# Routing's running sums on TensorE, and three reordered steps, in an attention and expert kernel

## The chip, the cores and the metric

The kernel runs on one core of a Trainium2 chip. A core has TensorE (PE in the profile, with its weight loads as PEld), VectorE (DVE), ScalarE (ACT), GpSimd (POOL) and SyncE (SP), which here issues most of the DMA transfers. The metric is the device time of one execution in microseconds.

## The reference

Eight images are each run through an attention of 8 heads (576 tokens, 64 channels a head) with an additive bias per head, and the result goes through a layer of 8 experts, of which each token takes one.

```python
scores = scale * np.matmul(q, k.transpose(0, 1, 3, 2))
h = np.maximum(x @ w1 + b1, 0.0)          # x from the distance of two positions
scores = scores + (h @ w2).transpose(2, 0, 1)[None]
attn = np.exp(scores - scores.max(-1)); attn = attn / (attn.sum(-1) + 1e-9)
out = attn @ v                            # reshaped to 4608 tokens x 512
...
logits = x @ w_gate + modality_bias[modality_id]
e_idx = np.argmax(logits, axis=1)
gate_w = softmax(logits)[arange(N), e_idx]
out[e_idx == e] = gate_w * (relu(x @ w1[e]) @ w2[e])   # for each expert e, F = 1024
```

## The kernel before

The program has three stages. The **table stage** (to about 66 us) computes the attention's bias for every distance: 32 blocks of hidden values (rows of `relu`, made by VectorE at L185 and ScalarE at L183), a product with `w2` on TensorE (L193), a copy out of the accumulator (`bias_put`, L209 on ScalarE) into a ring of four buffers, and a transfer to the table (SP's queue, L212). Among the blocks, a list of steps prepares the first pair of heads: `turn` (L378, VectorE) transposes q and k, and `split` (L385, L386) divides each into an upper part, ScalarE's cast, and a lower part, a subtraction that reads that cast. `SPLIT0 = (6, 10)` names the blocks behind which the two splits of pair 0 are issued.

The **attention** runs 32 pairs of heads, four to an image, one after the other, and each in five units of 128 (the last 64) query rows. What is issued in a unit is written out by hand in `ORDER`, one string per unit, a letter per step: S scores (L402) with VectorE's reduction for the row minimum (L416), e and f the exponentials of the two heads (ScalarE, L431), t and T the transposes of the exponentials of heads 1 and 2 (L446) from the block scored two units before, a, A, b, c the products with v (L500), R the transposes of the remainders (L474), X and B one step each of the routing. t writes the accumulator bank `eps_716`, T `eps_717`; the copy ("take") from the bank to `eT` is ScalarE's (L331) where `ON_ACT` names it (among others e11, e20, e21, e30: block and head) and VectorE's (L333) elsewhere. A digit behind a letter holds the take back by so many steps, but it is issued before its bank is written again. In unit 4, t and T handle block 2 (e20, e21); in unit 0 of the next pair, e30 and e31; in unit 1, block 4 (L452, bank 716). Every engine runs its instructions in the order in which they are issued.

The **routing** of an image runs as a list of steps spread over the next image's four pairs. I number an image's pairs 4k to 4k+3; the routing of the image before takes place from unit 4 of pair 4k to the end of pair 4k+3. Of interest here: in pair 4k+2 `s_top` in unit 0 (bias, maximum, subtraction, L784 to L787), `s_onehot` in unit 1 (L793 to L803), `s_rank` in unit 2 (each token's place among those of its expert: a product of the one-hot rows with a triangle of ones, and a product of running sums over the five blocks of rows with a matrix of ones, L816 and L817), then `s_gate` (L807 to L812) and in unit 3 `s_pos` (L828, L830), whose places GpSimd's scatter reads. The step of the last image runs at the start of the third stage.

The **expert layers** (from about 614 us) gather the tokens of each expert and run the two products.

The change touches `split`, `ORDER[4]`, `s_top`, `s_onehot`, `s_gate`, `s_rank` and `s_pos`.

Of the kernel before, what the change touches and what calls it, by code (L numbers as in the profile page):

```python
# [11 lines left out]
F32 = mybir.dt.float32  # L12
BF16 = mybir.dt.bfloat16
F32R = mybir.dt.float32r
I32 = mybir.dt.int32
AF = mybir.ActivationFunctionType
ALU = mybir.AluOpType
# [4 lines left out]
P = 128  # L22
S = 576
# [6 lines left out]
E = 8  # L30
# [78 lines left out]
class Attn:  # L109
# [270 lines left out]
    def split(self, n, part):  # L380

        nc = self.nc
        x, cols = (self.kT, slice(0, NK)) if part else (self.qT, slice(NK, NK + NQ))
        hi, lo = self.QK[n % 2][:, 0, cols], self.QK[n % 2][:, 1, cols]
        nc.scalar.copy(hi, x)  # L385
        nc.gpsimd.tensor_tensor(lo, x, hi.bitcast(F32), op=ALU.subtract)  # L386

    def scores(self, n, c):

# [127 lines left out]
    def first_steps(self, route):  # L517
# [31 lines left out]
    )  # L549

    def attention(self):
# [64 lines left out]
    def route_setup(self, cp):  # L616

        tc, nc, io = self.tc, self.nc, self.io
        B = self.B
        NC = 5 * B  # L620
        self.n_tab = -(-self.n_tok // TS) * TS + TS
        self.xg = self.dp.tile([(E + 1) * self.n_tab, XW], F32, name="xg")

        self.ones = cp.tile([P, P], BF16, name="ones")
        nc.gpsimd.memset(self.ones, 1.0)
        self.wgb = cp.tile([P, NP, 2, 16], F32, name="wgb")
        nc.gpsimd.memset(self.wgb, 0.0)

        self.lt4 = cp.tile([P, P], F32, name="lt4")
        nc.gpsimd.memset(self.lt4[:, 64:P], 0.0)  # L630
        self.rec = cp.tile([P, 5, H], F32, name="rec")
        nc.gpsimd.memset(self.rec, 1.0)
        self.oh = cp.tile([P, 6, E], F32, name="oh")
        nc.gpsimd.memset(self.oh, 0.0)
        self.ohb = cp.tile([P, 2, 6, E], BF16, name="ohb")
        nc.gpsimd.memset(self.ohb, 0.0)
        yield
        self.base = cp.tile([P, E], F32, name="base")
        nc.sync.dma_start(self.base, io["c_ebase"].to_broadcast([P, E]))
        yield  # L640
        blank = cp.tile([P, 2, XW], F32, name="blank")
        nc.gpsimd.memset(blank[:, :, 0:DM], 0.0)
        nc.gpsimd.memset(blank[:, :, DM:XW], float(self.n_tok))
        self.blank = blank
        self.gi = cp.tile([P, 5, 4], F32, name="gi")
        nc.gpsimd.memset(self.gi, 0.0)
        self.ids = cp.tile([P, NC], F32, name="ids")
        nc.sync.dma_start(self.ids, io["c_ids"])
        yield
        self.valid = cp.tile([P, 5], F32, name="valid")  # L650
        nc.sync.dma_start(self.valid, io["c_valid"])
        yield
        self.rev = cp.tile([P, E], F32, name="rev")
        nc.sync.dma_start(self.rev, io["c_rev"].to_broadcast([P, E]))
        yield
        wg = io["moe_w_gate"]
        for h in range(2):
            sl = slice(64 * h, 64 * h + 64)
            nc.sync.dma_start(
                self.wgb[sl, :, h, 0:E], wg.rearrange("(p a d) e -> a d p e", a=2, d=D)[h]  # L660
            )
            yield

        x0, x1 = self.xrb

        m2 = x0[:, 0 : 2 * NC].bitcast(I32).rearrange("p (b c w) -> p b c w", b=B, c=5)
        nc.gpsimd.memset(m2, 0)
        yield
        mid = io["moe_modality_id"].bitcast(I32)
        for c in range(4):  # L670
            nc.sync.dma_start(
                m2[:, :, c, :],
                mid.rearrange("(b s) -> b s", s=2 * S)[:, 2 * P * c : 2 * P * c + 2 * P].rearrange("b (p w) -> p b w", p=P),
            )
        yield
        nc.sync.dma_start(
            m2[0:64, :, 4, :], mid.rearrange("(b s) -> b s", s=2 * S)[:, 1024 : 2 * S].rearrange("b (p w) -> p b w", w=2)
        )
        yield
        tri = x1[:, 0:P]  # L680
        nc.sync.dma_start(tri, io["c_tri"])
        yield
        mb = x1[:, P : P + 2 * E].rearrange("p (a e) -> p a e", a=2)
        nc.sync.dma_start(
            mb.rearrange("p a e -> p (a e)"),
            io["moe_modality_bias"].rearrange("a (o e) -> o (a e)", o=1).to_broadcast([P, 2 * E]),
        )
        yield
        yield
        self.tri = cp.tile([P, P], BF16, name="tri")  # L690
        nc.gpsimd.tensor_copy(self.tri, tri)
        mf, m1 = x0[:, 2 * NC : 3 * NC], x0[:, 3 * NC : 4 * NC]
        nc.gpsimd.tensor_copy(mf, m2.rearrange("p b c w -> p (b c) w")[:, :, 0])
        nc.gpsimd.tensor_scalar(m1, mf, -1.0, 1.0, op0=ALU.mult, op1=ALU.add)
        self.mbias = cp.tile([P, NC, E], F32, name="mbias")
        yield
        t0 = x0[:, 4 * NC : 12 * NC].rearrange("p (n e) -> p n e", e=E)
        for a, (dst, mk) in enumerate(((t0, m1), (self.mbias, mf))):
            nc.gpsimd.tensor_tensor(
                dst,  # L700
                mk.rearrange("p (n o) -> p n o", o=1).to_broadcast([P, NC, E]),
                mb[:, a : a + 1, :].to_broadcast([P, NC, E]),
                op=ALU.mult,
            )
        yield
        nc.gpsimd.tensor_tensor(self.mbias, self.mbias, t0, op=ALU.add)

    def route_steps(self, b):
        nc, rt = self.nc, self.rt
        xT = [self.xT.pop(NP * b + p) for p in range(NP)]  # L710
        sums = [self.sums.pop(NP * b + p) for p in range(NP)]
        rec, oh = self.rec, self.oh
        C5 = [P, 5, E]
        st = {}

        def bc(t):
            return t.rearrange("p (c o) -> p c o", o=1).to_broadcast(C5)
# [64 lines left out]
        def s_top():  # L782
            lg = st["lg"]
            nc.vector.tensor_tensor(lg, lg, self.mbias[:, 5 * b : 5 * b + 5, :], op=ALU.add)  # L784
            mx = rt.tile([P, 5], F32, tag="mx", name=f"mx{b}")
            nc.vector.tensor_reduce(mx, lg, axis=AX.X, op=ALU.max)
            nc.vector.tensor_tensor(lg, lg, bc(mx), op=ALU.subtract)  # L787
            st["mx"] = mx

        def s_onehot():  # L790
            lg, mx = st["lg"], st["mx"]

            nc.vector.scalar_tensor_tensor(  # L793
                oh[:, 0:5, :], lg, 0.0, self.rev.rearrange("p (o e) -> p o e", o=1).to_broadcast(C5), op0=ALU.is_ge, op1=ALU.mult
            )
            nc.vector.tensor_reduce(mx, oh[:, 0:5, :], axis=AX.X, op=ALU.max)
            nc.vector.tensor_tensor(oh[:, 0:5, :], oh[:, 0:5, :], bc(mx), op=ALU.is_equal)
            nc.vector.tensor_tensor(oh[:, 0:5, :], oh[:, 0:5, :], bc(self.valid), op=ALU.mult)

            ohb = self.ohb  # L800
            nc.gpsimd.tensor_copy(ohb[:, 0, 0:5, :], oh[:, 0:5, :])
            for k in range(1, 6):
                nc.vector.tensor_tensor(ohb[:, 1, k, :], ohb[:, 1, k - 1, :], oh[:, k - 1, :], op=ALU.add)  # L803

        def s_gate():
            lg = st["lg"]
            nc.scalar.activation(lg, lg, AF.Exp)  # L807
            gt = rt.tile([P, 5], F32, tag="gt", name=f"gt{b}")
            nc.vector.tensor_reduce(gt, lg, axis=AX.X, op=ALU.add)
            nc.vector.tensor_scalar(gt, gt, 1e-9, None, op0=ALU.add)  # L810
            nc.vector.reciprocal(self.gi[:, :, 0], gt)
            nc.vector.tensor_copy(self.gi[:, :, 1], self.ids[:, 5 * b : 5 * b + 5])  # L812

        def s_rank():
            ps = self.xbank()[:, 0 : 6 * E].rearrange("p (c e) -> p c e", e=E)
            nc.tensor.matmul(ps, self.tri, self.ohb[:, 0], start=True, stop=False)  # L816
            nc.tensor.matmul(ps, self.ones, self.ohb[:, 1], start=False, stop=True)  # L817
            rk = rt.tile(C5, F32, tag="rk", name=f"rks{b}")
            bb = self.base.rearrange("p (o e) -> p o e", o=1)
            nc.vector.tensor_tensor(rk, ps[:, 0:5, :], bb.to_broadcast(C5), op=ALU.add)  # L820
            nc.vector.tensor_tensor(self.base, self.base, ps[:, 5, :], op=ALU.add)
            nc.vector.tensor_tensor(rk, rk, oh[:, 0:5, :], op=ALU.mult)
            st["rk"] = rk

        def s_pos():
            rk = st["rk"]
            pf = rt.tile([P, 5], F32, tag="pf", name=f"pf{b}")
            nc.vector.tensor_reduce(pf, rk, axis=AX.X, op=ALU.add)  # L828
            pos = rt.tile([P, 5], I32, tag="pos", name=f"pos{b}", bufs=2)
            nc.vector.tensor_copy(pos, pf)  # L830
            st["pos"] = pos

        def s_rows(c):
# [611 lines left out]
```

## Time and profile before

| | |
|---|---|
| median of 3 runs | 1062.39 us |
| lowest and highest | 1062.15 and 1063.95 us |
| the profiled execution's own time | 1062.4 us |
| its span in the trace | 1060.5 us |
| granted TensorE clock, share of full speed | 0.998 |
| busy, share of the span: PE, DVE, ACT, POOL | 95%, 70%, 63%, 29% |

The profile shows one execution. The span goes from the first to the last instruction of the trace and is 1.9 us shorter than the execution's own time. A row of a timeline groups neighbouring instructions of one kind: start, time from the first's start to the last's end, what they are, their count, and in brackets the idle time before them with what ended it. Rows overlap a little, since an instruction starts before the one before it has drained.

### The profile page before, as it was taken

The page shows a single profiled execution, that of the slowest core. Times are in us where ns is not written, and L with a number is a line of the kernel's source. Part 1 is how long each engine was busy: PE and PEld are TensorE (multiplying, and loading weights), DVE is VectorE, ACT ScalarE, POOL GpSimd, SP SyncE. Part 2 cuts the span into 40 slices and gives each one's busy share as a digit, 9 for nine tenths or more (in the row PEclk, how much of TensorE's full clock was granted, in tenths as well). Part 3 has the DMA queues.
Part 4 walks back from the last instruction along what each step waited for, and adds up shares of the span by engine and source line. Part 5 has one row for each costly group of instructions (what it writes and reads, how often), then busy time and mean ns, then how long its engine had stood idle before and what let it go on. Part 6 is the DMA issues. An engine that isn't in the chain of part 4 may idle for free. (4 is left out here: it accounts for less than half of the span.)

```text
span 1060.5 us, 22805 instructions
## 1 busy us (share of the span) xinstructions
PE 1011.3 (95%) x8388; PEld 801.6 (76%) x8388; DVE 742.7 (70%) x1566; ACT 666.9 (63%) x1284; POOL 304.4 (29%) x489
## 2 busy tenths in 40 slices
PE   6879999999999989999999999999999999999997
PEld 2357776767677767677676789999999999888896
DVE  7886678787787787877879676785556655554544
ACT  6777776777777767677676664455555545454544
POOL 1612333526335253352443411530010111111011
PEclk9999999999999999999999999999999999999999
DMA  6977723234242333343234410122113821152410
GB/s 151 191 158 141 190 54 71 62 66 102 47 78 69 69 76 69 58 93 65 58 74 131 137 41 30 61 86 70 41 41 133 297 67 46 65 184 73 166 42 24
DMA packets 225465, 97.52 MB, mean 92 GB/s; under 512 B 201262, under 2 KB 201646, under 8 KB 225346
## 3 DMA queue, kind: packets, MB, share of 16 engines
q1 hardware_dynamic: 219330, 76.96, 30.5%
q0 software_dynamic: 5920, 19.03, 5.0%
q8 instruction: 68, 1.11, 0.4%
q14 instruction: 51, 0.42, 0.1%
q10 hardware_dynamic: 96, 0.00, 0.0%
HBM read 134.94 MB, written 23.90 MB: 150 GB/s over the span
## 5 line engine op out<-in xcount | busy, mean ns | idle before, releaser
L431 ACT ACTIVATE Eb<-Eb,mn 128x576 f32<-128x576 f32 x288 | 221.7, 771 | 66.4 <-DVE mn L416 66.3
L416 DVE CUSTOM_DVE_ANT_0 Eb<-sps,NBm 128x576 f32<-128x576 f32 x256 | 183.6, 754 | 62.7 <-PE sps L402 53.8
L402 PE MATMUL sps<-QK 64*128 64x288 f32 (+1 forms) x1728 | 171.2, 309 | 2.3 <-DVE mn L416 2.0
L402 PEld LDWEIGHTS sps<-QK 64*128 64x128 f32 (+1 forms) x1728 | 133.8, 185 | 46.1 <-DVE mn L416 15.6
L1166 PE MATMUL p<-QK,w1hi 128*128 128x256 f32 x1136 | 160.9, 284 | 0.0
L446 PE MATMUL eps<-idf,Eb 128*128 128x128 f32 x1024 | 147.7, 279 | 10.6 <-DVE eT L333 8.2
L1169 DVE SCALAR_TENSOR_TENSOR hl<-p,hh 128x512 fp32r<-128x512 f32 x72 | 49.7, 691 | 148.5 <-ACT hh L1168 148.4
L1166 PEld LDWEIGHTS p<-QK,w1hi 128*128 128x128 f32 x1136 | 147.0, 192 | 2.9 <-issue 1.8
L500 PE MATMUL xps<-eT,vraw 128*64 128x288 f32 x1024 | 147.1, 412 | 0.0
L446 PEld LDWEIGHTS eps<-idf,Eb 128*128 128x128 f32 x1024 | 111.3, 140 | 41.4 <-issue 17.7
L1192 POOL DMA_INDIRECT out<-mo,idt x36 | 40.1, 1113 | 317.1 <-ACT QK L1149 234.1
L1168 ACT ACTIVATE hh<-p 128x512 fp32r<-128x512 f32 x72 | 43.1, 599 | 119.9 <-PE p L1166 113.8
L331 ACT ACTIVATE eT<-eps 128x512 f32<-128x512 f32 x160 | 95.0, 593 | 34.1 <-PE eps L446 25.5
L1183 PE MATMUL p<-w2hi,hh 128*128 128x512 f32 x288 | 114.2, 396 | 0.0
L1183 PE MATMUL p<-w2hi,hl 128*128 128x512 f32 x288 | 112.5, 391 | 0.0
L436 POOL COPY rem<-Eb 128x128 f32<-128x128 f32 x128 | 37.5, 294 | 248.2 <-ACT Eb L431 245.2
L500 PEld LDWEIGHTS xps<-eT,vraw 128*64 128x64 f32 x1024 | 65.3, 137 | 53.5 <-issue 19.6
L1129 DVE TENSOR_TENSOR w2lo<-NBm,w2hi 128x1024 fp32r<-128x1024 f32 x72 | 88.2, 1225 | 16.2 <-ACT w2hi L1128 16.2
L333 DVE COPY eT<-eps 128x512 f32<-128x512 f32 x128 | 87.1, 681 | 11.8 <-PE eps L446 11.5
L1166 PE MATMUL p<-QK,w1lo 128*128 128x256 f32 x568 | 91.3, 283 | 0.0
L1129 DVE TENSOR_TENSOR w1lo<-NBm,w1hi 128x1024 fp32r<-128x1024 f32 x72 | 83.2, 1220 | 0.0
L1191 ACT ACTIVATE mo<-p,gates 128x512 f32<-128x512 f32 x36 | 24.8, 690 | 89.4 <-PE p L1183 75.2
(211 smaller groups left out, 1646.2 us busy)
## 6 DMA issues: line engine op xcount, KB each, us to landing
NBm<-moe_w SPq DMA_DIRECT2D x23, 2048.0 KB
NBm<-moe_w SPq DMA_DIRECT2D x44, 1024.0 KB
NBr<-xg SPq DMA_DIRECT2D x20, 516.0 KB
kraw<-k SPq DMA_DIRECT2D x128, 72.0 KB
NBm<-xTb SPq DMA_DIRECT2D x32, 288.0 KB
vraw<-v SPq DMA_DIRECT2D x64, 128.0 KB
xg<-blank SPq DMA_DIRECT2D x9, 516.0 KB
qraw<-q SPq DMA_DIRECT2D x64, 72.0 KB
```

What stands on the lines that cost most here:

```text
L331: self.nc.scalar.activation(out, ps, AF.Copy, scale=scale)
L333: self.nc.vector.tensor_copy(out, ps)
L402: nc.tensor.matmul(self.sps[h][:, half, 0:HS], QK[o, q, qs], QK[o, k, HS * half : HS * half + HS], start=i == 0, stop=i == 2, skip_group_c ...
L416: nc.vector.tensor_tensor_reduce(out=e.rearrange("p (t w) -> p t w", t=2), in0=self.sps[h][:, :, 0:HS], in1=nb.rearrange("p (t w) -> p t w ...
L431: self.nc.scalar.activation(e, e, AF.Exp, bias=mn, scale=-1.0, accum_out=sm)
L446: nc.tensor.transpose(ps[:, k, :], e[:, part, P * k : P * k + P], self.idf)
L500: nc.tensor.matmul(ps[o, :], v[:, h, k, :], self.eT[:, h, k, sl], start=half == 1 and k == 0, stop=half == 0 and k == 3, tile_position=(0, ...
L1129: self.nc.vector.tensor_tensor(l, w, h.bitcast(F32), op=ALU.subtract)
L1166: nc.tensor.matmul(ps[:, a, :], w[:, c, fs], x[:, c, :], start=i == 0, stop=i == len(ops) - 1)
L1168: nc.scalar.activation(hh[:, sl, :], ps, AF.Relu)
L1169: nc.vector.scalar_tensor_tensor(hl[:, sl, :], ps, 0.0, hh[:, sl, :].bitcast(F32), op0=ALU.max, op1=ALU.subtract)
L1183: nc.tensor.matmul(ps, h[:, f, sl], m[:, f, :], start=i == 0, stop=i == len(ops) - 1)
```

## The change

Four things are changed. The lower parts of pair 0 are computed by VectorE instead of GpSimd, at the same place in the program. In unit 4 of every pair the transposes of head 2 are issued before those of head 1. In the routing, the five running sums of the one-hot rows and their cast are removed: the last product of the one-hot step writes bf16 itself, and the rank is one matmul with the triangle and five with the matrix of ones, the k-th adding block k's counts to the columns of all later blocks. The exponential of the logits moves from the gate's step to the maximum's. And the places are cast to integers by GpSimd, not by VectorE.

```diff
@@ split
-        nc.gpsimd.tensor_tensor(lo, x, hi.bitcast(F32), op=ALU.subtract)
+        (nc.gpsimd if n else nc.vector).tensor_tensor(lo, x, hi.bitcast(F32), op=ALU.subtract)
@@ ORDER
-        "B S t2 V T2 X e",
+        "B S T2 V t2 X e",
@@ route_setup
-        self.ohb = cp.tile([P, 2, 6, E], BF16, name="ohb")
+        self.ohb = cp.tile([P, 6, E], BF16, name="ohb")
@@ s_top
             st["mx"] = mx
+            st["eg"] = eg = rt.tile(C5, F32, tag="eg", name=f"eg{b}")
+            nc.scalar.activation(eg, lg, AF.Exp)
@@ s_onehot
-            nc.vector.tensor_tensor(oh[:, 0:5, :], oh[:, 0:5, :], bc(self.valid), op=ALU.mult)
-
-            ohb = self.ohb
-            nc.gpsimd.tensor_copy(ohb[:, 0, 0:5, :], oh[:, 0:5, :])
-            for k in range(1, 6):
-                nc.vector.tensor_tensor(ohb[:, 1, k, :], ohb[:, 1, k - 1, :], oh[:, k - 1, :], op=ALU.add)
+            nc.vector.tensor_tensor(self.ohb[:, 0:5, :], oh[:, 0:5, :], bc(self.valid), op=ALU.mult)
@@ s_gate
-            lg = st["lg"]
-            nc.scalar.activation(lg, lg, AF.Exp)
+            lg = st["eg"]
@@ s_rank
-            nc.tensor.matmul(ps, self.tri, self.ohb[:, 0], start=True, stop=False)
-            nc.tensor.matmul(ps, self.ones, self.ohb[:, 1], start=False, stop=True)
+            ohb = self.ohb
+            nc.tensor.matmul(ps, self.tri, ohb, start=True, stop=False, skip_group_check=True)
+            for k in range(5):
+                nc.tensor.matmul(
+                    ps[:, k + 1 : 6, :],
+                    self.ones,
+                    ohb[:, k : k + 1, :].to_broadcast([P, 5 - k, E]),
+                    start=False,
+                    stop=k == 4,
+                    skip_group_check=True,
+                )
-            nc.vector.tensor_tensor(rk, rk, oh[:, 0:5, :], op=ALU.mult)
+            nc.vector.tensor_tensor(rk, rk, self.ohb[:, 0:5, :], op=ALU.mult)
@@ s_pos
-            nc.vector.tensor_copy(pos, pf)
+            nc.gpsimd.tensor_copy(pos, pf)
```

How the issued order moves, at three places. First TensorE in unit 4 of a pair and at the start of the next pair's first scores (the rows with a minus are the kernel before, with a plus the change; `eps_716` and `eps_717` are the banks of heads 1 and 2):

```order
 L402 MATMUL sps_714<-QK_72 128x288 x6
-L446 MATMUL eps_716<-idf,Eb 128x128 x4
-L446 MATMUL eps_717<-idf,Eb 128x128 x4
+L446 MATMUL eps_717<-idf,Eb 128x128 x4
+L446 MATMUL eps_716<-idf,Eb 128x128 x4
 L402 MATMUL sps_714<-QK_73 128x288
```

The two groups of four transposes change places; the first transposes of the next pair (e30, again bank 716) follow behind its first scores.

Then ScalarE, from unit 4 of a pair 4k+1 to unit 0 of pair 4k+2. Before (L431 are exponentials, L331 takes from the banks, the last one the remainders'):

```order
L431 ACTIVATE Eb,sums_1718<-Eb,mn_3_1_1862 128x576
L331 ACTIVATE eT<-eps_716 128x4x128
L431 ACTIVATE Eb,sums_1718<-Eb,mn_4_0_1899 128x576
L331 ACTIVATE eT<-eps_717 128x4x128
L331 ACTIVATE eT<-eps_716 128x4x128
L431 ACTIVATE Eb,sums_1921<-Eb,mn_0_0_1934 128x576
L331 ACTIVATE rT<-xps_78 128x512
```

And with the change:

```order
L431 ACTIVATE Eb,sums_1718<-Eb,mn_3_1_1862 128x576
L331 ACTIVATE eT<-eps_717 128x4x128
L431 ACTIVATE Eb,sums_1718<-Eb,mn_4_0_1899 128x576
L331 ACTIVATE eT<-eps_716 128x4x128
L790 ACTIVATE eg_1942<-lgs_1917 128x40
L331 ACTIVATE eT<-eps_716 128x4x128
L431 ACTIVATE Eb,sums_1921<-Eb,mn_0_0_1934 128x576
L331 ACTIVATE rT<-xps_78 128x512
```

The two takes of block 2 have changed places, so that both takes of bank 716 stand one behind the other, and the routing's exponential (L790) stands between them. In pairs without that step the order is the same without L790.

Last, VectorE in the table stage (L185 are hidden tiles, L386 the lower parts):

```order
 L185 TENSOR_SCALAR Eb<-xTb_94,xrb_89 128x576 x3
-L185 TENSOR_SCALAR eT<-xTb_94,xrb_89 128x576 x3
+L185 TENSOR_SCALAR eT<-xTb_94,xrb_89 128x576 x2
+L386 TENSOR_TENSOR QK_72<-qT,QK_72 128x640
+L185 TENSOR_SCALAR eT<-xTb_94,xrb_89 128x576
 L185 TENSOR_SCALAR Eb<-xTb_94,xrb_89 128x576
 L185 TENSOR_SCALAR eT<-xTb_94,xrb_89 128x576 x4
```

The lower part of q stands within the run of hidden tiles; that of k stands the same way four blocks further on.

## Rows read from the trace of the kernel before

**Rows 1.** Busy time by stretch: PE, PEld, DVE, ACT, POOL, clock, DMA share, GB/s.
```profile
32.00:48.00 16.00, 11.33 (x132) 4.84 (x129) 11.12 (x26) 9.86 (x15) 11.03 (x1) 1.00 1.10 186
208.56:276.82 68.26, 65.25 (x596) 47.75 (x596) 53.02 (x138) 48.82 (x115) 28.15 (x44) 1.00 0.35 71
614.50:1060.50 446.00, 438.04 (x3078) 397.20 (x3077) 265.78 (x352) 227.39 (x302) 69.22 (x128) 0.99 0.25 87
```

**Rows 2.** Waits of PE: total us, times, longest us.
```profile
PE xps L817 <- DVE ohb L803: 11.4, 7, 1.6
PE eps L446 <- DVE eT L333: 8.2, 18, 0.9
PE eps L446 <- ACT Eb L431: 2.1, 7, 0.3
```

**Rows 3.** ACT's timeline, unit 4 of an ordinary pair.
```profile
111.46 0.59 ACT L331 ACTIVATE eT<-eps 128x512 f32<-128x512 f32 x1
```

**Rows 4.** PE's timeline, unit 4 and behind it in three pairs.
```profile
109.54 1.06 PE L446 MATMUL eps<-idf,Eb 128*128 128x128 f32 x8 [0.16 <-DVE eT L333]
...
111.52 0.66 PE L446 MATMUL eps<-idf,Eb 128*128 128x128 f32 x4
...
225.44 1.09 PE L446 MATMUL eps<-idf,Eb 128*128 128x128 f32 x8
...
227.55 0.66 PE L446 MATMUL eps<-idf,Eb 128*128 128x128 f32 x4
...
228.92 0.64 PE L452 MATMUL eps<-idf,Eb 128*128 128x128 f32 x4
...
244.18 1.06 PE L446 MATMUL eps<-idf,Eb 128*128 128x128 f32 x8 [0.92 <-DVE eT L333]
...
246.61 0.66 PE L446 MATMUL eps<-idf,Eb 128*128 128x128 f32 x4
```

**Rows 5.** DVE's timeline, unit 0 of a pair 4k+2.
```profile
229.53 0.20 DVE L787 TENSOR_TENSOR lgs<-lgs,mx 128x40 f32<-128x40 f32 x1
```

**Rows 6.** ACT's timeline, the exponential of the logits and what follows.
```profile
238.40 0.22 ACT L807 ACTIVATE lgs<-lgs 128x40 f32<-128x40 f32 x1
238.53 0.76 ACT L431 ACTIVATE Eb<-Eb,mn 128x576 f32<-128x576 f32 x1
```

**Rows 7.** DVE's timeline, the end of the one-hot step in the same pair.
```profile
234.19 0.20 DVE L798 TENSOR_TENSOR oh<-oh,valid 128x40 f32<-128x40 f32 x1
234.43 2.41 DVE L803 TENSOR_TENSOR ohb<-ohb,oh 128x8 bf16<-128x8 bf16 x5
```

**Rows 8.** PE's timeline, the rank in the same pair.
```profile
235.07 0.19 PE L816 MATMUL xps<-ohb,tri 128*128 128x48 bf16 x1
...
237.00 0.71 PE L500 MATMUL xps<-eT,vraw 128*64 128x288 f32 x4
```

**Rows 9.** PE's timeline, the rank of the last image.
```profile
647.57 0.20 PE L816 MATMUL xps<-ohb,tri 128*128 128x48 bf16 x1
647.61 0.18 PE L817 MATMUL xps<-ohb,ones 128*128 128x48 bf16 x1
```

**Rows 10.** DVE's timeline, the cast of the places.
```profile
240.66 0.83 DVE L830 CAST pos<-pf 128x5 int32<-128x5 f32 x1
```

**Rows 11.** DVE's timeline in the table stage.
```profile
16.62 1.38 DVE L185 TENSOR_SCALAR eT<-xTb,xrb 128x576 f32<-128x576 f32 x3
...
21.19 2.11 DVE L185 TENSOR_SCALAR rT<-xTb,xrb 128x576 f32<-128x576 f32 x1
```

**Rows 12.** ACT's timeline in the table stage: the cast of pair 0's q.
```profile
19.48 0.74 ACT L385 CAST QK<-qT 128x640 fp32r<-128x640 f32 x1
```

**Rows 13.** Line L1150: count, duration in ns (least, median, most), first and last start.
```profile
L1150 DVE TENSOR_TENSOR QK<-xps,QK x38: 672/685/693, 605.9 to 1049.2; 128x512 fp32r<-128x512 f32 x38
```

**Rows 14.** Line L803, the same columns.
```profile
L803 DVE TENSOR_TENSOR ohb<-ohb,oh x40: 166/168/1477, 166.2 to 647.2; 128x8 bf16<-128x8 bf16 x40
```

**Rows 15.** POOL's timeline beside the sums of rows 7.
```profile
234.89 1.53 POOL L386 TENSOR_TENSOR QK<-qT,QK 128x640 fp32r<-128x640 f32 x1
```

## The prediction

> **What bounds the kernel now.** I began with the table by stretches [rows 1]. In the expert layers TensorE is busy 438.04 of 446.00 us, and in one image of the attention (four pairs, 208.56 to 276.82) 65.25 of 68.26 us: TensorE is the bound, and an edit to another engine is worth what TensorE waits less. In the middle of the table stage it is not (11.33 of 16.00 us); there the DMA engines are full, share 1.10, with the table being written out. Then I read what TensorE waits for [rows 2]: the rank's second matmul for VectorE's running sums, 11.4 us in 7 images (1.63 each); the transposes of a unit 4 for a VectorE copy, 8.2 us (0.92 seven times, in pairs 4k+2, and 0.16 eleven times); and 0.30 seven times in pairs 4k+3. An image idles 3.01 us, so the attention parts can't gain more than that per image, 21 us in all. The profiled execution's own time, 1062.4, is the median of the runs, so the sum needs no correction. A run can tell 0.2% (2.1 us) from no change.
>
> **Unit 4, head 2 first: the gain.** Today bank 716 is transposed first, and must be free of the copy before it; with 717 first that wait (0.14 of the 0.16 in ordinary pairs and in pairs 4k, 0.92 in 4k+2, 0.30 in 4k+3) goes, because 717's last copy, ScalarE's, ends earlier.
>
> **Unit 4: what is late next.** The copies now end on bank 716, and unit 0 writes 716 again (e30). Before, 716 was copied first and the second copy, 717's, was the late one; the new order gives 716 that late slot. The second copy starts at 111.46 and lasts 0.59 [rows 3], so 716 is free at 112.05 plus about 0.1 for the release: 2.61 after the transposes began at 109.54 [rows 4]. TensorE comes to e30 at 111.52, after 1.98: a new wait of 0.63 in an ordinary pair. In pair 4k+1 it comes 2.11 after (225.44, 227.55): 0.50. In 4k+2 2.43 after (244.18, 246.61), and 4k+3 has the same steps between: 0.18 each. In pairs 4k eight routing matmuls stand between, and nothing is left. Ordinary pairs 0 to 3 thus lose 0.63 − 0.14 = 0.49 each, +2.0; the last pair has little behind it, I put +0.4 (between 0 and 0.6).
>
> **The early exponential.** It leaves the gate step and is issued with the maximum's subtraction. On ScalarE's queue it now stands in pair 4k+2's unit 0, ahead of the copy of e30, and behind that are the next exponentials and the copy of rT. It needs VectorE's subtraction, 229.53 + 0.20 = 229.73 [rows 5]. An exponential of this size hands on to the next instruction after 0.13 (238.40 to 238.53) [rows 6]; with 0.05 to start it, e30's copy runs from 229.91 to 230.51, and the transposes of e40, which wait for its bank and began at 228.92 [rows 4], begin at 230.61. That is +1.69, of which 0.50 is the wait above: **+1.17 more per image**. Low end 0 (if the subtraction came earlier), high end 1.7. What ScalarE has queued there is then late too, but it idles later in the pair, and I charge no more.
>
> **Running sums on TensorE.** VectorE's last one-hot product ends at 234.39, and the five adds then take 2.41 us from 234.43 [rows 7]; the rank's first matmul starts at 235.07 and the next work, the values' product, at 237.00 [rows 8]: 1.93 us for the step. Now the product writes bf16 itself and is ready at 234.39, before TensorE arrives, so 235.07 stays and six matmuls follow each other. In the last image the two of today started 38 ns apart (647.57, 647.61) [rows 9], with a weight load between them. Five further starts at 0.04 to 0.10, and 0.11 for the last, give 0.3 to 0.6: I take 0.43, a gain of **1.50 per image**. Bounds: 1.62 at 38 ns; at 0.19 each, a matmul's full duration [rows 8], six in a row take 1.1 and the gain is 0.8. By the page "TensorE: Matmul & The Clock Gate" of the Trainium skill (Back-to-back issue gap) a pair of weight load and matmul with 128 columns is about 81 ns; by that figure the gain would be 1.41 and the sum, as an estimate, 0.6 us higher. No run here shows it for so few columns streamed, so I keep the row.
>
> **The cast to GpSimd.** VectorE is rid of 0.83 us [rows 10] per image beside TensorE's work; GpSimd's split of the next pair's keys now waits up to 0.8 us behind the cast, but its result is only read by the next pair's scores, several us later. Both nothing. The cast of the one-hots that GpSimd no longer does hid behind scores. In the last image four extra matmuls cost 0.15.
>
> **The sum of the attention.** Per image: −0.14 (4k) + 0.50 + 1.17 (4k+1) − 0.92 + 0.18 − 1.50 (4k+2) − 0.30 + 0.18 (4k+3) = −0.83, seven times −5.8. With +2.0, +0.4 and +0.15: **−3.25 us**.
>
> **The first pair's lower parts.** These are now VectorE's, in the middle of the table stage. VectorE comes to the first after two of the three tiles that begin at 16.62 and take 1.38 together [rows 11], at 17.5; but ScalarE's cast that it needs starts at 19.48 and ends at 20.22 [rows 12]. It waits 2.7 us, with all later table tiles behind it, and then works itself: a 128x512 subtraction takes 0.69 there [rows 13], so 640 columns are about 0.8. Against that, one tile at 21.19 took 2.11 us [rows 11] where the three above took 0.46 each, while GpSimd did this very subtraction; that 1.6 comes back. Net +1.9 us for blocks 7 to 10. The second waits for ScalarE's cast of the keys, itself later, and takes 0.75: by my replay about 1.5 more, +3.5 at the writes of block 11. How much of it the transfers queued by then absorb, no row tells; behind that point the DMA engines are full [rows 1], so what is lost there stays lost. I take **+2.7**, the middle of 1.9 and 3.5; ends 0 and 3.5.
>
> **Sum:** 1062.4 − 3.25 + 2.7 = **1061.9 us**, no change that can be told.
>
> **The rivals.**
> *A, faster: the table stage swallows the delay.* If the writes at block 11 have enough queued, or later blocks idle anyway, only the attention counts: 1062.4 − 3.25 = **1059.2**. For it: TensorE idles nearly a third of the table stage. Against: a DMA share of 1.10 just behind the delay. 0.20.
> *B, faster: the exponential doesn't hold ScalarE.* If VectorE gets to the subtraction a microsecond earlier, 8.2 us come back: 1061.9 − 8.2 = **1053.7**. Against: in the rows before 229.53 VectorE works without a break on scores that need TensorE. 0.07.
> *C, slower: the six matmuls run one after another.* At 0.19 each the gain is 0.8 in place of 1.5, 4.8 us less in seven images: 1061.9 + 4.8 = **1066.7**. Every one of the six has its own weight load, and the loads must then fail to run ahead. Against: the 38 ns between today's two [rows 9], which also have one load each. 0.10.
> *D, slower: VectorE's one-hot products meet GpSimd's split.* Of the 40 adds the median takes 0.17 us and the longest 1.48 [rows 14], beside GpSimd's subtraction at 234.89 that takes 1.53 [rows 15]. The last product ends at 234.39, 0.5 us before it. With the cast of the one-hots gone from GpSimd the subtraction may start sooner; if it starts before the product, the product waits out 1.5 us and ends near 235.9. The rank, which TensorE wants at 235.07, is then 0.9 late: 7 times, 6.3 us, **1068.2**. What decides is which of the two starts first. The subtraction needs ScalarE's cast and a copy on GpSimd ahead of it, and neither moves earlier. 0.07. The page "SBUF — State Buffer" (Who interferes with whom) says that a VectorE instruction with two SBUF inputs is blocked by a GpSimd one that reads SBUF, for its whole length; the long add of this trace agrees.
>
> **How the numbers follow.** The forecast has 0.56, its own range 1059.6 to 1065.0: the table stage's term from 1.5 to 3.5 gives 1060.7 to 1062.7, the rank's gain between 1.62 and 1.3 moves that by −0.8 and +1.4, the small waits of unit 4 by −0.3 and +0.9. Of that 0.41 within 0.2% (1060.3 to 1064.5), 0.08 below, 0.07 above. Faster: 0.08 + 0.20 + 0.07 = 0.35. Same: 0.41. Slower: 0.07 + 0.10 + 0.07 = 0.24. The range takes in A and C, with some tenths for the small terms: 1058.2 to 1067.0. B and D (0.14) and a little at the ends stay out.
>
> **What would show it.** The rank's wait for VectorE gone and about 0.4 us from its first matmul to the next product. In unit 0 a new wait of the transposes, about 0.6 in ordinary pairs, for ScalarE's copy of bank 716. In unit 1 of pair 4k+2 (the line of the e40 transposes) a wait of a microsecond for ScalarE. In the table stage VectorE idle near 17.5 to 20.2 for ScalarE's cast, and the first scores of the attention 2 to 3 us later. The forecast is wrong if the attention's period per image is not about 67.4 us, or if the table stage ends at the same time as before or over 4 us later.

## The result, and the profile after

The changed kernel takes **1054.65 us** (median of 5 runs, 1052.09 to 1056.25) beside 1063.04 for the kernel before (1062.15 to 1064.00): a ratio of 0.9917, 95% interval 0.9902 to 0.9933, so 8.4 us or 0.8% faster. The prediction was 1061.9, with a range from 1058.2 to 1067.0. The forecast of no change and the range were both wrong; "faster" had a chance of 0.35, and no rival was this mechanism.

The profiled execution took 1052.23 us, its span is 1050.5. Busy time by stretch (the columns of [rows 1]; the second row is the same image):

```profile
32.00:48.00 16.00, 15.02 (x165) 7.33 (x160) 13.01 (x32) 12.22 (x18) 0.00 (x0) 1.00 0.96 185
210.84:277.19 66.35, 64.82 (x604) 47.69 (x600) 50.24 (x129) 48.55 (x115) 28.17 (x44) 1.00 0.36 73
614.50:1050.50 436.00, 428.10 (x2996) 387.57 (x2994) 257.26 (x338) 220.87 (x293) 68.73 (x127) 1.00 0.25 88
```

An image of the attention takes 66.35 in place of 68.26 us: 1.9 us less, where the prediction had 0.83. Seven images make 13.4 us; the table stage gives 1.0 back (first scores at 67.10 instead of 66.06), and the first five pairs and pairs 28 and 29 some 2.5, so that about 10 are left in this execution. What TensorE waits for in the attention (total, times, longest, beside [rows 2]):

```profile
PE eps L452 <- ACT eT L331: 7.1, 7, 1.0
...
PE eps L446 <- ACT eT L331: 5.5, 14, 0.6
```

The wait for VectorE's sums and those of unit 4 are gone, and both new waits that the prediction named have come, at the places it named: e30's transposes wait for the copy of bank 716, and e40's (L452) for the copy of e30 behind the early exponential. TensorE in pair 4k+1's end and pair 4k+2, to be read beside [rows 4, 8]:

```profile
228.11 0.66 PE L446 MATMUL eps<-idf,Eb 128*128 128x128 f32 x4 [0.34 <-ACT eT L331]
...
230.66 0.66 PE L452 MATMUL eps<-idf,Eb 128*128 128x128 f32 x4 [1.02 <-ACT eT L331]
...
236.85 0.19 PE L813 MATMUL xps<-ohb,tri 128*128 128x48 bf16 x1
236.88 0.27 PE L815 MATMUL xps<-ohb,ones 128*128 128x40 bf16 x5
237.07 1.19 PE L500 MATMUL xps<-eT,vraw 128*64 128x288 f32 x8
...
242.29 0.82 PE L402 MATMUL sps<-QK 128*128 128x288 f32 x5
242.95 1.03 PE L446 MATMUL eps<-idf,Eb 128*128 128x128 f32 x8
```

The values' product starts 0.22 us after the first of the rank's six matmuls, where it was 1.93. The transposes of unit 4 (242.95) follow the scores without a wait. ScalarE at the early exponential, beside [rows 6]:

```profile
227.48 0.58 ACT L331 ACTIVATE eT<-eps 128x512 f32<-128x512 f32 x1
229.89 0.24 ACT L790 ACTIVATE eg<-lgs 128x40 f32<-128x40 f32 x1 [1.83 <-DVE lgs L787]
230.03 0.58 ACT L331 ACTIVATE eT<-eps 128x512 f32<-128x512 f32 x1
```

ScalarE stands idle for 1.83 us before a 0.24 us exponential, with the copy of e30 queued behind it.

**A wait is longer than the idle time in its row.** TensorE's idle time is counted from the modelled end of the last matmul, but a following matmul can start before that end. From the first of unit 4's six scores to its transposes, with no wait, is 0.87 us; it was 1.03 in a pair 4k+1 before, whose row shows no idle time at all, 1.97 in 4k+2 (row: 0.92) and 1.34 in 4k+3 (row: 0.30). The scores before the transposes of [rows 4], in 4k+1 and 4k+2:

```profile
224.41 1.04 PE L402 MATMUL sps<-QK 128*128 128x288 f32 x6
...
242.21 1.05 PE L402 MATMUL sps<-QK 128*128 128x288 f32 x6
```

The waits were thus 0.16 to 0.18 longer than their rows say. Distances of starts give the image's account:

| place | before | after | change | predicted |
|---|---|---|---|---|
| unit 4, scores to transposes: 4k, 4k+1, 4k+2, 4k+3 | 1.19, 1.03, 1.97, 1.34 | 1.00, 0.88, 0.87, 0.87 | −1.90 | −1.36 |
| unit 0, scores to e30: 4k+2, 4k+3, 4k (next) | 1.00, 0.99, 1.00 | 1.41, 1.14, 1.14 | +0.72 | +0.86 |
| pair 4k+2, e31 to e40 | 0.44 | 1.61 | +1.18 | +1.17 |
| pair 4k+2, rank to the values' product | 1.93 | 0.22 | −1.71 | −1.50 |
| pair 4k+2, the scores behind that product | 1.19 | 0.99 | −0.19 | 0 |

The lines add up to −1.90, against −0.83 predicted. They say where the time went, not which part of the change moved it; for that the parts were run alone.

### The profile page after: what moved, and what is told of

The parts are those of the page before. It is cut to its first block, busy times and chain, and to the rows that moved or that the text cites. A ratio compares the mean times of both kernels' runs of the same rounds, so it can differ in the third digit from the quotient of the medians.

```text
span 1050.5 us, 22776 instructions
## 1 busy us (share of the span) xinstructions
PE 1010.1 (96%) x8420; PEld 802.2 (76%) x8420; DVE 722.2 (69%) x1520; ACT 664.4 (63%) x1284; POOL 286.3 (27%) x487
## 4 chain that ended last, share of the span: by engine, by line
PE 84%; ACT 4%; DVE 2%; issue 1%; DMA 0%; POOL 0%; SPq 0%; POOLq 0%; ACTq 0%; DVEq 0%
PE p L1171 19%; PE p L1188 19%; PE xps L500 13%; PE sps L402 12%; PE eps L446 10%; PE xps L491 3%; ACT eT L331 2%; PE eps L452 2%; PE xps L1151 2%; ACT Eb L431 1%; PE xps L843 1%; PE xps L474 1%; PE xps L745 1%; DVE Eb L416 1%; PE p L1370 1%
## 5 line engine op out<-in xcount | busy, mean ns | idle before, releaser
L431 ACT ACTIVATE Eb<-Eb,mn 128x576 f32<-128x576 f32 x288 | 221.2, 769 | 47.5 <-DVE mn L416 41.1
L416 DVE CUSTOM_DVE_ANT_0 Eb<-sps,NBm 128x576 f32<-128x576 f32 x256 | 183.7, 755 | 73.3 <-PE sps L402 69.7
L436 POOL COPY rem<-Eb 128x128 f32<-128x128 f32 x128 | 37.8, 296 | 296.6 <-ACT Eb L431 270.9
L331 ACT ACTIVATE eT<-eps 128x512 f32<-128x512 f32 x160 | 94.5, 590 | 27.7 <-PE eps L446 25.0
```

The source lines that it names most:

```text
L331: self.nc.scalar.activation(out, ps, AF.Copy, scale=scale)
L416: nc.vector.tensor_tensor_reduce(out=e.rearrange("p (t w) -> p t w", t=2), in0=self.sps[h][:, :, 0:HS], in1=nb.rearrange("p (t w) -> p t w ...
L431: self.nc.scalar.activation(e, e, AF.Exp, bias=mn, scale=-1.0, accum_out=sm)
```

## The experiments

The change has five parts, not four as it says above: the lower parts, the order of unit 4, the rank without running sums, the early exponential, and the cast of the places. The period is the distance of the first scores of pairs 9 and 13, from one profile each; the ratio is to the kernel before, run beside it on the same chip.

| run | what | median, us | ratio and 95% interval | period, us |
|---|---|---|---|---|
| before | | 1062.5 to 1063.1 | | 68.25 |
| the change | all parts | 1054.65 | 0.9917 (0.9902 to 0.9933) | 66.35 |
| 1 | order of unit 4 alone | 1061.66 | 0.9993 (0.9977 to 1.0008) | 67.61 |
| 2 | rank alone | 1046.44 | 0.9839 (0.9823 to 0.9855) | 65.97 |
| 3 | first pair's lower parts alone | 1064.51 | 1.0012 (0.9999 to 1.0024) | 68.23 |
| 4 | the change, exponential back in the gate | 1045.08 | 0.9818 (0.9800 to 0.9836) | 65.13 |
| 5 | early exponential alone | 1075.03 | 1.0112 (1.0095 to 1.0129) | 69.76 |
| 6 | places cast by GpSimd alone | 1060.67 | 0.9973 (0.9959 to 0.9986) | 67.56 (pairs 5 to 9) |
| 7 | rank alone, the sums kept but unread | 1061.43 | 0.9981 (0.9971 to 0.9990) | 68.06 |
| 8 | parts chosen | 1042.11 | 0.9798 (0.9782 to 0.9814) | 65.16 |
| 9 | the kernel before, one split moved | 1060.30 | 0.9970 (0.9959 to 0.9980) | 68.00 |
| 10 | parts chosen, places by GpSimd | 1040.71 | 0.9794 (0.9773 to 0.9815) | 64.90 |
| 11 | the change, lower parts on GpSimd | 1050.84 | 0.9888 (0.9868 to 0.9908) | 66.34 |

**1. The order of unit 4 alone.**

```diff
-        "B S t2 V T2 X e",
+        "B S T2 V t2 X e",
```

> The kernel before with the order of unit 4 alone. Theory W (a wait of TensorE begins before the idle time that its row shows, because the row counts idle time only from the modelled end of the last matmul; it is read from the distance of starts): unit 4 gives back 0.15 us in pair 4k+1, 1.10 in 4k+2, 0.46 in 4k+3, and unit 0 takes 0.41, 0.15 and 0.15; the image's period goes from 68.26 to about 67.1, and with some 2 us lost in the first and last pairs the time falls by about 6. Rival I (the idle columns are the whole waits, as the prediction took them): period about 67.8, time 1 us less.

The period is 67.61, nearer to rival I (67.8) than to W's 67.1, and the time falls by 0.7 us, within its interval. W's reading of the waits holds (the distance in pair 4k+1 shrinks by 0.15 though its row showed no idle time, as W said); what failed is that the order alone doesn't end the wait of pair 4k+2. PE's timeline there:

```profile
243.62 1.05 PE L402 MATMUL sps<-QK 128*128 128x288 f32 x6
245.07 1.09 PE L446 MATMUL eps<-idf,Eb 128*128 128x128 f32 x8 [0.39 <-ACT eT L331]
```

Of 1.10 us 0.58 remain (1.45 in place of 0.87 from start to start): with the sums and the cast still on VectorE, bank 717's copy is late too. ScalarE makes it at 244.44, behind an exponential for which it stood idle for 0.77 us until VectorE's reduction was done. So about half of that wait in the changed kernel was ended by something else. Runs 8 and 10 below tell by what: with this order and the rank without sums the distance is 1.04, and with the cast on GpSimd too it is 0.87.

**2. The rank alone.** The changed kernel's `s_onehot` and `s_rank` in the kernel before; all else as it was.

```diff
-            nc.vector.tensor_tensor(oh[:, 0:5, :], oh[:, 0:5, :], bc(self.valid), op=ALU.mult)
-            nc.gpsimd.tensor_copy(ohb[:, 0, 0:5, :], oh[:, 0:5, :])
-            for k in range(1, 6):
-                nc.vector.tensor_tensor(ohb[:, 1, k, :], ohb[:, 1, k - 1, :], oh[:, k - 1, :], op=ALU.add)
+            nc.vector.tensor_tensor(self.ohb[:, 0:5, :], oh[:, 0:5, :], bc(self.valid), op=ALU.mult)
```

> The kernel before with the rank by six matmuls and without the five sums and their cast; the exponential stays in the gate's step, the order of unit 4 and both places of the subtraction and the cast as before. Theory W: the rank's step shrinks from 1.93 to 0.22 us and the scores behind it lose a hidden wait of 0.19: 1.90 per image, period 66.36, time 13 us less. The prediction's price: 1.50 per image, 10.5 us less. A third reading: VectorE, rid of 2.4 us, also reaches the copy that unit 4 of pair 4k+2 waits for sooner; then that wait of about 1.1 us shrinks too, the period falls below 66, and the order of unit 4 is worth less beside it.

16.1 us faster, about twice what the whole change gains, and the third reading is the one that holds: pair 4k+2 shrinks from 19.06 to 16.75, by 2.31. Of this 1.71 is the rank's step, 0.19 the scores behind it, and 0.41 the wait of unit 4, which this part doesn't touch:

```profile
231.61 0.19 PE L812 MATMUL xps<-ohb,tri 128*128 128x48 bf16 x1
231.64 0.27 PE L814 MATMUL xps<-ohb,ones 128*128 128x40 bf16 x5
231.84 1.19 PE L500 MATMUL xps<-eT,vraw 128*64 128x288 f32 x8
...
238.39 1.06 PE L446 MATMUL eps<-idf,Eb 128*128 128x128 f32 x8 [0.52 <-DVE eT L333]
```

**7. The rank alone, with the sums kept.** Cast and sums write a spare tile that nobody reads; the rank no longer needs them.

```diff
+            nc.gpsimd.tensor_copy(self.spare[:, 0, 0:5, :], oh[:, 0:5, :])
+            for k in range(1, 6):
+                nc.vector.tensor_tensor(self.spare[:, 1, k, :], self.spare[:, 1, k - 1, :], oh[:, k - 1, :], op=ALU.add)
```

> The kernel of the second experiment (rank by six matmuls) with the cast and the five sums kept on GpSimd and VectorE, written to a tile that nobody reads. If the gain beyond the rank's own step (0.19 in the scores behind it, 0.41 in the wait of unit 4) is VectorE's 2.4 us, both come back and the period is about 66.5 in place of 65.95, the time about 4 us over that kernel's. If it is the rank's earlier end, the period stays at 65.95.

Far more comes back than any reading said: 15 of the 16 us, and the period is 68.06. TensorE is past the rank in 0.22 us, and then waits for VectorE all the same, 2 us further on. Its timeline in pair 4k+2, and VectorE's beside it:

```profile
235.56 0.19 PE L817 MATMUL xps<-ohb,tri 128*128 128x48 bf16 x1
235.59 0.27 PE L819 MATMUL xps<-ohb,ones 128*128 128x40 bf16 x5
235.79 1.19 PE L500 MATMUL xps<-eT,vraw 128*64 128x288 f32 x8
237.91 0.40 PE L402 MATMUL sps<-QK 64*128 64x288 f32 x1 [0.93 <-DVE mn L416]
238.58 1.06 PE L402 MATMUL sps<-QK 64*128 64x288 f32 x11 [0.28 <-DVE mn L416]
...
244.43 1.06 PE L446 MATMUL eps<-idf,Eb 128*128 128x128 f32 x8 [0.92 <-DVE eT L333]
```

```profile
234.78 2.32 DVE L803 TENSOR_TENSOR spare<-spare,oh 128x8 bf16<-128x8 bf16 x5
237.08 0.76 DVE L416 CUSTOM_DVE_ANT_0 Eb<-sps,NBm 128x576 f32<-128x576 f32 x1
...
237.77 0.75 DVE L416 CUSTOM_DVE_ANT_0 Eb<-sps,NBm 128x576 f32<-128x576 f32 x1
```

The reductions of unit 2's scores (L416) stand behind the sums, and the next scores need their banks: 0.93 + 0.28 us. Unit 4's wait is back at 0.92. GpSimd's cast of the one-hots came back with the sums and was not tried by itself; what TensorE waits for in these rows is VectorE's. So **the gain is VectorE's 2.4 us, not TensorE's wait for the rank.** Ending that wait alone is worth 0.2 per image (68.25 to 68.06); VectorE's time is worth the other 2.1. VectorE's queue was the path here, and TensorE's wait at the rank only the first place where it showed.

**9. The kernel before with one split moved.** In pairs 4k+2 alone:

```diff
+    ORDER2 = "S t1 k e T2 X B 0 f C b"
...
+                late = u == 2 and n >= NP and n % NP == 2
+                for op in (self.ORDER2 if late else self.ORDER[u]).split():
```

> The kernel before with one step moved: in unit 2 of pairs 4k+2 the split of the next pair's q stands behind the rank's steps, so that GpSimd's subtraction no longer runs beside VectorE's five sums. If the long add of 1.48 us comes from that meeting, the five sums take about 1.1 us in place of 2.41, TensorE's wait for them falls from 1.63 to about 0.3, and the period from 68.26 to between 66.5 and 67; that is, over half of the rank's gain was to be had without touching the rank. If the long add has another cause, sums and period stay.

The meeting is shown, and the expected gain did not come. The timelines of VectorE, GpSimd and TensorE in pair 4k+2:

```profile
234.15 1.10 DVE L806 TENSOR_TENSOR ohb<-ohb,oh 128x8 bf16<-128x8 bf16 x5
...
237.90 1.42 DVE L813 TENSOR_SCALAR gt<-gt 128x5 f32<-128x5 f32 x1
239.36 0.19 DVE L814 RECIPROCAL gi<-gt 128x5 f32<-128x5 f32 x1
239.46 0.13 DVE L815 COPY gi<-ids 128x5 f32<-128x5 f32 x1
239.50 0.68 DVE L333 COPY eT<-eps 128x512 f32<-128x512 f32 x1
...
240.32 0.61 DVE L833 CAST pos<-pf 128x5 int32<-128x5 f32 x1
```

```profile
237.73 1.57 POOL L386 TENSOR_TENSOR QK<-qT,QK 128x640 fp32r<-128x640 f32 x1 [3.09 <-ACT QK L385]
...
239.49 1.41 POOL L386 TENSOR_TENSOR QK<-kT,QK 128x576 fp32r<-128x576 f32 x1
```

```profile
235.31 0.18 PE L820 MATMUL xps<-ohb,ones 128*128 128x48 bf16 x1 [0.32 <-DVE ohb L806]
...
240.24 0.66 PE L446 MATMUL eps<-idf,Eb 128*128 128x128 f32 x4 [0.85 <-DVE eT L333]
```

The sums now take 1.10 us and the rank waits 0.32, as expected. But GpSimd's subtraction, now from 237.73 to 239.30, met an addition of the gate step on 5 columns (L813), which took 1.42 us in place of 0.17; the copy behind it came late, and TensorE lost 0.85 us in unit 3. The period fell by 0.25 only. Moving the subtraction moved the hold: the sums became 1.31 us shorter, and L813 1.25 us longer.

**5. The early exponential alone, and 4, the change without it.** In 5 the exponential moves to the maximum's step, in 4 it moves back:

```diff
+            st["eg"] = eg = rt.tile(C5, F32, tag="eg", name=f"eg{b}")
+            nc.scalar.activation(eg, lg, AF.Exp)
```

> The kernel before with the exponential of the logits moved to the maximum's step, and nothing else. If it holds ScalarE by itself, the transposes of e40 in unit 1 of pair 4k+2 wait for ScalarE's copy of e30, about 1.2 us or more per image (period 69.5, time 8 us more): the order of unit 4 is not needed for it. If it only hurts behind the new order, the period stays 68.26.

> The changed kernel with the exponential of the logits back in the gate's step. If the early exponential holds ScalarE's copy of e30, and that the transposes of e40, the wait of 1.0 us in unit 1 of pair 4k+2 goes, 1.18 per image, the period falls from 66.33 to 65.15 and the time by 8 us against the changed kernel, to about 1045. If what the early copy frees is only held up later, the period falls by less than half of that.

Alone it costs 1.51 us per image (68.25 to 69.76) and 12.1 us, in this wait of PE:

```profile
PE eps L452 <- ACT eT L331: 10.2, 7, 1.5
```

Taken out of the changed kernel it gives 1.22 per image back (66.35 to 65.13) and, by the two ratios, 0.99% or 10.5 us; the row of e40's transposes is gone from PE's waits. It needs no new order to hurt: the exponential waits for VectorE's subtraction, and ScalarE's copies wait behind the exponential. This is the part that the change should not have made.

**6. The places cast by GpSimd, alone.**

```diff
-            nc.vector.tensor_copy(pos, pf)
+            nc.gpsimd.tensor_copy(pos, pf)
```

> The kernel before with the cast of the places on GpSimd alone. The prediction's price is nothing: period 68.26, time within 1 us. If VectorE's 0.83 us, which lie two units before the copy that unit 4 of pair 4k+2 waits for, matter, that wait of 1.1 us falls by up to 0.8, and the time by up to 5.6 us.

Not nothing: pair 4k+2 takes 18.37 in place of 19.06 in four of the seven images, and unit 4's wait falls from 0.92 to 0.25. Behind the cast on VectorE's queue stand the reductions and copies of the unit, and the copy that unit 4 waits for. Line L830 (count, least, median and most duration in ns), before and in this run:

```profile
L830 DVE CAST pos<-pf x8: 171/824/856, 172.4 to 660.0; 128x5 int32<-128x5 f32 x8
```

```profile
L830 POOL CAST pos<-pf x8: 188/188/192, 172.0 to 659.1; 128x5 int32<-128x5 f32 x8
```

TensorE at unit 4 in this run:

```profile
173.53 1.03 PE L402 MATMUL sps<-QK 128*128 128x288 f32 x6
174.81 0.41 PE L446 MATMUL eps<-idf,Eb 128*128 128x128 f32 x2 [0.25 <-DVE eT L333]
```

On VectorE the cast of five columns took 0.83 where it ran beside GpSimd's split of k (240.03 to 241.47), and ended with it, at 241.49; in the last image, with nothing beside it, it took 0.17. In run 9, where that split ends earlier, at 240.90, the cast takes 0.61 and ends at 240.93. In the other three images TensorE runs slower for some 3 us (below), so that the timed gain is only 0.3%.

**3. The lower parts alone, and 11, the change without them.**

```diff
-        nc.gpsimd.tensor_tensor(lo, x, hi.bitcast(F32), op=ALU.subtract)
+        (nc.gpsimd if n else nc.vector).tensor_tensor(lo, x, hi.bitcast(F32), op=ALU.subtract)
```

> The kernel before with the first pair's lower parts on VectorE alone. If the changed kernel's early start (its clock rose to full speed 2 us sooner) had nothing to do with the change, the first scores come 1.0 to 2.0 us later than before (66.1), less where the clock rises early. If the delay is the prediction's 2.7, they come at 68.8. The period of an image stays 68.26.

> The changed kernel with the first pair's lower parts back on GpSimd. The traces so far have the first scores at 64.9 to 67.3 us with GpSimd (seven kernels) and at 66.6 to 69.2 with VectorE (three), a difference of means of 1.3. By that the time falls by 1 to 1.5 us against the changed kernel, to about 1053; by the prediction's term it falls by 2.7, to 1052; with no cost of the part it stays.

Alone the part costs 1.3 us (−0.1 to +2.6); the two ratios of the change with it and without differ by 0.29%, 3.1 us, and their intervals (0.9902 to 0.9933, 0.9868 to 0.9908) overlap a little. The first scores come at 66.6 to 69.2 us in the three kernels with it, and at 64.9 to 67.3 in ten without. So the part costs something like 1 to 3 us, and these runs don't fix it better. VectorE in the changed kernel, beside [rows 11]:

```profile
19.41 0.82 DVE L386 TENSOR_TENSOR QK<-qT,QK 128x640 fp32r<-128x640 f32 x1 [2.06 <-ACT QK L385]
...
23.85 0.48 DVE L185 TENSOR_SCALAR rT<-xTb,xrb 128x576 f32<-128x576 f32 x1
...
27.82 0.76 DVE L386 TENSOR_TENSOR QK<-kT,QK 128x576 fp32r<-128x576 f32 x1 [1.34 <-ACT QK L385]
```

Both idle times for ScalarE's casts, the price of the work (0.82, 0.76) and the tile that is short again (0.48 in place of 2.11) are there as forecast; the first idle time is 2.06 where the prediction had 2.7.

**8 and 10. The parts that pay.** The rank by six matmuls, the exponential in the gate, the lower parts on GpSimd, and the new order only where it gains; in 10 also the cast on GpSimd.

```diff
+    ORDER4 = "B S T2 V t2 X e"
...
+                turned = u == 4 and NP <= n < n_pair - NP and n % NP != 1
+                for op in (self.ORDER4 if turned else self.ORDER[u]).split():
```

> The rank by six matmuls, exponential in the gate's step, lower parts on GpSimd, places cast by VectorE, and the new order of unit 4 only in pairs 4 to 27 without pairs 4k+1. From the rows of the first, second and fourth experiment the order then gives back 0.19 in 4k, 0.72 in 4k+2 and 0.46 in 4k+3 and takes 0.15 twice: period 64.9, and no loss in the first and last four pairs. About 1040 us, 6 below the second experiment's kernel. If the wait in unit 0 comes back in another pair, not below the fourth's 1045.

> The kernel of the eighth experiment with the places cast by GpSimd. Alone, that cast took 0.69 us off pair 4k+2 by shortening the wait of unit 4. Behind the new order that wait has already gone, so I expect the period to stay within 0.1 of 65.1 and the time within 2 us of 1042. If VectorE is still what unit 4 waits for, another 0.2 per image goes.

Period 65.16 and 64.90 (expected 64.9, and then "within 0.1, or another 0.2": it was the latter, pair 4k+2 going from 16.25 to 16.03). **1040.71 us** is 2.1% below the kernel before and beats the change by 1.2%. In run 10 the image's 64.90 us hold 64.70 us of busy TensorE:

```profile
206.53:271.43 64.90, 64.70 (x603) 47.69 (x599) 50.24 (x129) 48.52 (x115) 28.17 (x44) 1.00 0.37 75
```

## Why the prediction was wrong

**The step that failed is the running sums, "a gain of 1.50 per image".** I priced them by TensorE's step alone: from the rank's first matmul to the next product, 1.93 us to 0.43. That TensorE's part was mis-sized is the small error (1.71, more than the bound of 1.62: the matmuls follow each other faster than the 38 ns taken from the last image, as the last section shows). The large one is the question itself: the sums stood on VectorE's queue, and "are they waited for" was the wrong test. Run 2 gave 2.31 per image, 0.8 more than I had, or 5.7 us in seven images, and run 7 shows that only 0.2 of it is the wait that I priced; all the rest is VectorE's 2.4 us, which without the rank's wait would have come out at the next scores. The trace of before had it: the sums of [rows 7] end at 236.84, and what follows them on VectorE are the reductions that free the banks for unit 3's scores.

```profile
236.82 0.76 DVE L416 CUSTOM_DVE_ANT_0 Eb<-sps,NBm 128x576 f32<-128x576 f32 x1
```

**"The cast to GpSimd: both nothing" failed for the same reason.** I called 0.83 us "beside TensorE's work", and never asked who comes after it on VectorE. Run 6 gives 0.69 in each image where TensorE's clock stays. A duration of 0.83 for five columns, where the same line's least was 0.17, was a sign by itself that it was held.

**"With 717 first that wait goes" was right in the changed kernel for another reason.** By run 1 the order alone ends only 0.52 of the 1.10 us in pair 4k+2; VectorE's relief did the rest (runs 8 and 10). The gain of the order alone is 0.64 per image (68.25 to 67.61), where I had 0.50. I had read the idle times of the rows as the whole waits, some 0.16 too short each. Net of the new waits the gain lay mostly in pairs 4k+3 (0.33) and 4k+1 (0.15), and of the 4.5 us in seven images some 2 were lost again in the first five pairs and in pairs 28 and 29.

**Right, with its size:** the new wait of e30 (0.41 in pair 4k+1 against 0.50, 0.15 against 0.18), and the early exponential behind the new order, +1.18 against +1.17, with the wait at the line and unit named. Rival B falls: ScalarE was held in every image.

**Right in kind, uncertain in size:** the table stage, +2.7 in the sum. The changed kernel's own profile has +1.04, with a TensorE whose products became short some 2 us earlier (below); the timed runs say 1.3 and 3.1.

**The other rivals.** A would have been right if the table term had vanished; it has not, and 1059.2 was not the time. C falls: the six matmuls take 0.22 to the next product. D did not happen: in the changed kernel GpSimd's subtraction starts at 236.61, behind the last product of the one-hots (235.96 + 0.20). But its mechanism is what made the sums and the cast dear (1.3 of 2.4 us and 0.66 of 0.83): its price stood under a rival, and belonged into the sum as a gain.

Put together with the parts as measured alone, −0.64 for the order, −2.28 for the rank, +1.51 for the exponential, −0.69 for the cast: −2.1 per image, near the measured −1.9. The parts share one wait (unit 4 of pair 4k+2), so they don't add up exactly. What stays open is the table stage's term between 1 and 3 us, and 0.7 us that the change loses in pair 28 (there TensorE waits 0.37 for GpSimd's copy of a remainder, L436); no run separates these.

## What to carry to other kernels

Before pricing the removal of work by the wait that it ends, ask who stands behind that work on its own engine: a queue that is late shows its lateness at the first wait and, when that is gone, at the next one. The test is cheap: keep the work and remove only the wait; if the time hardly moves, the work was the cost. And an instruction put earlier in a strictly ordered queue must have its input by then, since all that is queued behind it pays, here 12 us for a 0.24 us exponential.

## What the runs showed of the hardware that I had not expected

**Small VectorE instructions are held by GpSimd's long ones, also with one input.** An addition of 128x8 took 1.48 us beside GpSimd's 1.53 us subtraction and 0.17 without; a `tensor_scalar` of 128x5 took 1.42 in place of 0.17 (run 9), a cast of 128x5 0.83 or 0.61 in place of 0.17. All of them ended within 0.03 us of GpSimd's instruction: the price is what is left of that one, however small the held one is. The Trainium skill's page "SBUF — State Buffer" (Who interferes with whom) says so of both kinds: two SBUF inputs contend with a GpSimd read, and casts and `tensor_scalar` can through their two-port modes, for the whole instruction. The traces agree, and the reduction L416, with one of its two inputs in the accumulator, stayed at 0.76 us beside such a subtraction in the changed kernel.

**Pairs of a 128-column weight load and a tiny matmul start 25 ns apart.** The last five matmuls of the rank take 0.27 us from the first's start to the last's end (row 236.88 above) and 0.166 to 0.181 each, which leaves 25 ns from start to start, for 8 to 40 bf16 columns. The figure of 81 ns per pair that the Trainium skill's page "TensorE: Matmul & The Clock Gate" (Back-to-back issue gap) gives is for 128 columns streamed; no run here has such pairs.

**The rate of TensorE scatters single profiles.** In the table stage a 512-column product takes 1.06 us up to a start at 13.54 us in the kernel before and 10.89 in the changed one, and 0.59 to 0.62 from 14.56 and 12.46 on; both began at 8.8 to 8.9, so that the changed profile was 1.1 us ahead at the fourth block (13.43 beside 14.56). The granted clock of both stretches reads 1.00; that the long ones ran at the lower of the clock's two levels (1.2 and 2.4 GHz) is read from the durations alone and not shown. In run 6 the granted clock does show it: in three images it falls to 0.50, the lower level, after the wait of 1.62 to 1.66 us for the sums. The granted clock over that stretch, in an image where it stayed and in one where it fell (columns of [rows 1]):

```profile
167.50:171.50 4.00, 3.29 (x29) 2.06 (x30) 3.83 (x16) 2.32 (x6) 0.54 (x2) 1.00 0.02 4
235.20:239.60 4.40, 3.83 (x23) 2.18 (x22) 4.13 (x17) 2.32 (x6) 0.42 (x3) 0.61 0.00 0
```

In the second the eight products behind the wait take 2.05 us in place of 1.19, and the image loses 1.4 us. The kernel before has the same wait in each image and its profile shows no such fall; why it came in three images stays open.
